# Token order for the row buffers of a gated memory-transformer and FFN kernel: one 128-partition transfer per group in place of two with an outer dimension of 4

## The chip, the core and the metric

The kernel runs on one core of one Trainium2 chip. The metric is device time in microseconds (us) of one execution; several executions are run and their median is taken. All times below are us unless marked otherwise.

The core has a matrix engine (PE, whose weight loads the profile lists as PEld), three engines for elementwise work (DVE, ACT, POOL) and a synchronization engine (SP). DMA transfers are issued here from SP's queue (q1 in the profile) and from ACT's queue (q10); 16 DMA engines carry them out.

## What is computed

Sizes: 2048 tokens of width 640, in 64 segments of 32; 8 memory rows; 32 heads of 192; FFN width 1536. Activations and weights are bf16. Cut to what matters:

```python
g = sigmoid((x * gate_w).sum(-1, keepdims=True))
mem, outs = mem0, []
for s in range(64):
    h = concat([mem, x[32 * s:32 * s + 32]])          # 40 rows
    q, k, v = h @ Wq, h @ Wk, h @ Wv                  # per head
    p = softmax(where(mask, q @ k.T * scale, -1e9))
    o = (p @ v) @ Wo
    mem = o[:8]                                       # feeds the next segment
    outs.append(o[8:])
a = concat(outs)
b = (gelu(x @ w_gate) * (x @ w_up)) @ w_down
out = g * a + (1 - g) * b
```

The memory makes the 64 segments a chain: no segment can start its queries before the last one has its output.

## The kernel before

Everything is written out in program order by a small scheduler (`_Sched`, L50): `add` puts an operation on one engine's list, works out from byte regions what it must wait for, and `emit_stream` (L197) writes each list. An engine's list runs in order, so an operation that waits holds everything behind it on that engine; a DMA's issue belongs to the list of the engine that issues it.

**Stages.** First the FFN for all tokens (L775 to L787), its result stored to a scratch tensor in HBM in plain rows of 128 tokens by one transfer each (L771). Then the queries and keys of the last 8 tokens of every segment, the "left" tokens, which do not depend on the memory, for all segments at once (L796 to L823). Then the 64 segments (`segment`, L1025), each following the list `PROG` (L464): four "octets" of heads, with Q and K projections (`cmode`, L867, matmul L871), evacuation by ACT (L877), transposes (L883), scores and softmax (`scores`, L922: matmul L937, maximum L952, subtraction L954 on DVE, exponential L956 on ACT), V projection (`v_oct`, L898, matmul L905), P transposes, PV and the output projection (`wo_part`, L1011, matmul L1020). A segment ends with the evacuation of the new memory (L1070).

**Weights.** They do not all fit in SBUF. A planner at build time (L501 to L510) keeps 60 of the 84 pieces resident and streams 24 pieces per segment through a ring of five slots, issued in order from SP (`issue_ring`, L544; `piece`, L556) as soon as a slot's last reader is done. Resident pieces whose place is in use early are loaded later: one class after the FFN (L789), another during segment 0 (`load_late`, L573).

**Rows.** Segments come in groups of four (128 tokens; g is the group, q = s % 4 the place in it). One buffer `rowb`, 128 partitions of one token row each (1280 bytes), serves in turn

- the x rows of the next group, loaded in the segment with q = 1 after its second K projection (L1041), transposed in the one with q = 3 (`x_group_transposes`, L658) into `Hx` and used for the gate (`gate_group`, L667) and, segment by segment, by POOL's copies into the segment's input `Hb` (`x_copy`, L699: L701 and L702);
- the FFN rows of this group, loaded in the segment with q = 3 after its third K projection (L1050);
- the output of this group, mixed by DVE in the next group's first segment (`out_group`, L843: L845, L848, L850) and stored from there (`out_store`, L854). The last group's store ends the kernel.

The rows stand in a permuted order: partitions 0 to 95 hold the first 24 tokens of each of the four segments, partitions 96 to 127 the left 8 of each. So `perm_dma` (L638) moves a group by two transfers on ACT's queue, issued at L640, whose HBM side has the outer dimension 4 (segments), then 24 or 8 tokens, then the row. `Hx` and `aT4` (the transposed attention output, filled at L1072 and L1074) have the same order in their columns, and the left tokens of a group are the 32 adjacent columns `Hx[:, k, 96:128]`, which the V projection uses directly (L914).

POOL's list interleaves the copies of the left queries and keys into each octet's Q and K (`left_fill`, L834: L835 and L839) with the x copies.

Of the kernel before, what the change touches and what calls it, by code (L numbers as in the profile page):

```python
# [221 lines left out]
def _build(nc, A_x, A_mem0, A_Wq, A_Wk, A_Wv, A_Wo, seg_len, w_gate, w_up, w_down,  # L222
           gate_w, out, opts=None):
    opts = dict(opts or {})
    Bsz, S, Dm = A_x.shape
    M = A_mem0.shape[1]
    H, Dh = A_Wq.shape[1], A_Wq.shape[2]
    Df = w_gate.shape[1]
    L = int(seg_len)
    assert Bsz == 1 and M == 8 and L == 32 and Dh == 192  # L230
    assert Dm % 128 == 0 and H % 4 == 0 and S % 128 == 0 and Df % 128 == 0
    KT = Dm // 128
# [7 lines left out]
    R = L + M  # L240
    XA = L - M
# [15 lines left out]
    S_ = _Sched(nc)  # L257
    Rg = S_.region
    AUXQ = opts.get("auxq", "act")

    x2 = A_x[0]
    out2 = out[0]
    b_scr = nc.dram_tensor("ffn_b_scratch", (S, Dm), BF, kind="Internal").ap()
# [5 lines left out]
    def al(n):  # L269
        return (n + 63) // 64 * 64  # L270

    wsA = {}
    wsB = {}
    wsA["H"] = al(2 * KT * R * 2)
    wsA["Hx"] = al(KT * 128 * 2)
    wsA["gcol"] = al(2 * 4 * 4)
    wsA["gwT"] = al(KT * 2)
    wsA["ident"] = al(128 * 2)
# [46 lines left out]
    o = wsA_base - wsB_total  # L325
# [6 lines left out]
    o = wsA_base  # L332
    wsA_off = {}
# [3 lines left out]
    o = ffn_base  # L337
# [4 lines left out]
    def bview(o, nbytes, plo=0, phi=128):  # L342
        return arena[plo:phi, o // 2:(o + nbytes) // 2]

    def fview(o, nbytes, plo=0, phi=128):
        return arena[plo:phi, o // 2:(o + nbytes) // 2].bitcast(F32)

    def sreg(o, nbytes, plo=0, phi=128):
        return Rg("sb", o, o + nbytes, plo, phi)

    o_H = wsA_off["H"]
    Hb = [bview(o_H + b * KT * R * 2, KT * R * 2).rearrange("p (k r) -> p k r", r=R) for b in range(2)]
# [2 lines left out]
    o_Hx = wsA_off["Hx"]  # L355
    Hx = bview(o_Hx, KT * 256).rearrange("p (k t) -> p k t", t=128)
    r_Hx = sreg(o_Hx, KT * 256)
    gcol = fview(wsA_off["gcol"], 32)
    r_gcol = [sreg(wsA_off["gcol"] + 16 * b, 16) for b in range(2)]
    gwT = bview(wsA_off["gwT"], KT * 2)  # L360
# [11 lines left out]
    r_mle = sreg(wsA_off["mle"], 32)  # L372
    rowb = bview(wsA_off["rowb"], Dm * 2)
    r_rowb = sreg(wsA_off["rowb"], Dm * 2)
    r_rowbh = [sreg(wsA_off["rowb"], Dm * 2, 0, 4 * XA), sreg(wsA_off["rowb"], Dm * 2, 4 * XA, 128)]
    Qs = bview(wsB_off["Q"], 12 * R * 2).rearrange("p (s r) -> p s r", r=R)
    r_Qm = sreg(wsB_off["Q"], 8)
    r_Ql = sreg(wsB_off["Q"] + 8, 12 * R * 2 - 8)
# [28 lines left out]
    aT4 = bview(wsB_off["aT4"], KT * 256).rearrange("p (k t) -> p k t", t=128)  # L407
# [32 lines left out]
    r_ps = [Rg("ps", b, b + 1) for b in range(8)]  # L440
# [42 lines left out]
    for item in PROG:  # L483
        kind, i = item[0], item[1]
# [33 lines left out]
    o = ring_bytes  # L518
# [9 lines left out]
    o = ring_bytes  # L528
# [71 lines left out]
    def load_residents(cls):  # L600
        for key in order:
# [7 lines left out]
           reads=[r_ident], writes=[r_ident])  # L609
# [3 lines left out]
           reads=[r_e40], writes=[r_e40])  # L613
# [15 lines left out]
    for b in range(8):  # L629
        S_.add("dve", lambda e, b=b: e.memset(ps[:, b, :], 0.0), writes=[r_ps[b]])  # L630

    PP = (slice(0, 4 * XA), slice(4 * XA, 128))

    def rows(ap, g):
        v = ap[128 * g:128 * g + 128, :].rearrange("(s t) d -> s t d", t=L)
        return v[:, 0:XA, :], v[:, XA:L, :]

    def perm_dma(dst, src, reads, writes, sem, watch=False):  # L638
        for i in range(2):
            S_.add(AUXQ, lambda e, i=i: e.dma_start(dst(i), src(i)), reads=reads, writes=writes[i:i + 1],  # L640
                   dma_sem="%s%d" % (sem, i), watch=watch, name=sem)

    def ffn_x_load(blk):
        s = blk % 2
# [4 lines left out]
    S_.add("sp", lambda e: e.dma_start(mem0r[0:M, :], A_mem0[0]), writes=[r_mem0r], dma_sem="mem0")  # L649
    S_.add("sp", lambda e: e.dma_start(gwr[0:KT, :], gate_w.rearrange("(k p) -> k p", p=128)),  # L650
           writes=[r_gwr], dma_sem="gwr")
    perm_dma(lambda i: rowb[PP[i]], lambda i: rows(x2, 0)[i], [], r_rowbh, "rowb")
    ffn_x_load(0)
    S_.add("sp", lambda e: e.dma_start(wg_sb, w_gate.rearrange("(k p) f -> p k f", p=128)), writes=[r_wg], dma_sem="wg")
    S_.add("sp", lambda e: e.dma_start(wu_sb, w_up.rearrange("(k p) f -> p k f", p=128)), writes=[r_wu], dma_sem="wu")
# [3 lines left out]
    def x_group_transposes(g, bk):  # L659
        pv = psb(bk)  # L660
        S_.add("pe", [lambda e, k=k: e.transpose(pv[:, k * 128:(k + 1) * 128], rowb[:, k * 128:(k + 1) * 128], ident)
                      for k in range(KT)],
               reads=[r_rowb, r_ident], writes=[r_ps[bk]], name="xT g%d" % g)
        S_.add("dve", lambda e: e.tensor_copy(out=Hx, in_=pv[:, 0:KT * 128].rearrange("p (k t) -> p k t", t=128)),
               reads=[r_ps[bk]], writes=[r_Hx], name="xT evac g%d" % g)

    def gate_group(g, bk):  # L667
        b = g % 2
# [29 lines left out]

    def x_copy(s):  # L699
        nb, hx, q = s % 2, Hx, s % 4  # L700
        S_.add("pool", [lambda e: e.tensor_copy(out=Hb[nb][:, :, 0:XA], in_=hx[:, :, q * XA:(q + 1) * XA]),  # L701
                        lambda e: e.tensor_copy(out=Hb[nb][:, :, L:R], in_=hx[:, :, 4 * XA + q * M:4 * XA + (q + 1) * M])],  # L702
               reads=[r_Hx], writes=[r_Hxp[nb]], name="x copy s%d" % s)

    def ffn_transposes(blk):
# [146 lines left out]
               reads=[r_ps[bk], r_rowb, r_gcol[g % 2]], writes=[r_rowb], name="mix2 g%d" % g)  # L852

    def out_store(g):  # L854
        perm_dma(lambda i: rows(out2, g)[i], lambda i: rowb[PP[i]], [r_rowb], [], "outw", True)

    OB = 7
    misc = [0]
# [39 lines left out]
    def v_oct(s, o):  # L898
        hb = s % 2
        bank = misc_bank()  # L900
        left = s % 4 == 0
        bank2 = misc_bank() if left else None

        def mms(bk, lhs, k, g_):
            return [lambda e, j=j: e.matmul(  # L905
                ps[32 * j:32 * j + 32, bk, 0:384], lhs, g_[:, 384 * j:384 * (j + 1)],
                start=(k == 0), stop=(k == KT - 1), tile_position=(0, 32 * j)) for j in range(4)]

        for k in range(KT):
            g_, rg_ = piece(s, (2, o, k))  # L910
            S_.add("pe", mms(bank, Hb[hb][:, k, 0:L], k, g_),
                   reads=[rg_, r_Hm[hb], r_Hxp[hb]], writes=[r_ps[bank]], name="V s%d o%d k%d" % (s, o, k))
            if left:
                S_.add("pe", mms(bank2, Hx[:, k, 4 * XA:128], k, g_),  # L914
                       reads=[rg_, r_Hx], writes=[r_ps[bank2]], name="Vl s%d o%d k%d" % (s, o, k))
        S_.add("act", lambda e: e.activation(out=v_sb[o % NVB], in_=ps[:, bank, 0:384], func=ACTF.Copy),  # L916
               reads=[r_ps[bank]], writes=[r_v[o % NVB]], name="V evac s%d o%d" % (s, o))
        if left:
            S_.add("dve", lambda e: e.tensor_copy(out=vl_sb[o], in_=ps[:, bank2, 0:384]),
                   reads=[r_ps[bank2]], writes=[r_vl[o]], name="Vl evac s%d o%d" % (s, o))  # L920
# [104 lines left out]
    def segment(s):  # L1025
        g, q = s // 4, s % 4
        qkbank = {}
        for item in PROG:
            kind, i = item[0], item[1]
            if kind in ("q", "k"):  # L1030
                qkbank[kind] = misc_bank()
                cmode(s, "qk".index(kind), i, qkbank[kind])
                if kind == "q":
                    rows_evac(qkbank["q"])
                if kind == "k" and i == 0 and q == 0 and g > 0:
                    out_group(g - 1, misc_bank())
                if kind == "k" and i == 1:
                    if q == 0 and g > 0:
                        out_store(g - 1)
                    if q == 1 and g + 1 < NG:  # L1040
                        perm_dma(lambda j: rowb[PP[j]], lambda j: rows(x2, g + 1)[j], [], r_rowbh, "rowb")  # L1041
                    if q == 3 and g + 1 < NG:
                        x_group_transposes(g + 1, misc_bank())
                if kind == "k" and i == 2:
                    if s + 1 < NSEG:
                        x_copy(s + 1)
                    if q == 3:
                        if g + 1 < NG:
                            gate_group(g + 1, misc_bank())
                        perm_dma(lambda j: rowb[PP[j]], lambda j: rows(b_scr, g)[j],  # L1050
                                 [Rg("dr", 128 * g, 128 * g + 128)], r_rowbh, "rowb")
            elif kind == "tq":
                row_transp(s, 0, i)
                rows_evac(qkbank["k"])
            elif kind == "tk":
                row_transp(s, 1, i)
            elif kind == "sc":
                scores(s, i)
            elif kind == "v":
                v_oct(s, i)  # L1060
            elif kind == "pt":
                p_transp(s, i)
            elif kind == "pv":
                pv_oct(s, i)
            else:
                wo_part(s, item)
        O3 = ps[:, OB, 0:KT * R].rearrange("p (n r) -> p n r", r=R)
        if s + 1 < NSEG:
            nb = (s + 1) % 2
            S_.add("act", lambda e: e.activation(out=Hb[nb][:, :, XA:L], in_=O3[:, :, XA:L], func=ACTF.Copy),  # L1070
                   reads=[r_ps[OB]], writes=[r_Hm[nb]], name="mem evac s%d" % s)
        S_.add("dve", lambda e: e.tensor_copy(out=aT4[:, :, q * XA:(q + 1) * XA], in_=O3[:, :, 0:XA]),  # L1072
               reads=[r_ps[OB]], writes=[r_aT4], name="aT evac s%d" % s)
        S_.add("dve", lambda e: e.tensor_copy(out=aT4[:, :, 4 * XA + q * M:4 * XA + (q + 1) * M], in_=O3[:, :, L:R]),  # L1074
               reads=[r_ps[OB]], writes=[r_aT4], name="aT evac2 s%d" % s)

    stg_load(0)
# [84 lines left out]
```

## Time and profile before

| | |
|---|---|
| median of 3 runs | 2227.48 us |
| lowest, highest | 2223.69, 2227.95 us |
| span of the profiled execution, first to last instruction | 2220.5 us |
| median less span | 7.0 us |
| mean granted PE clock in the profile | 0.986 |
| bytes moved by DMA in the profile | 642.75 MB |

The profile records one execution; its own time is known by its span only, and what lies around the span (7.0 us) is taken from the median of the runs. Lines such as L640 are lines of the kernel. In the busy digits the span is cut into equal slices, and each digit is a share in tenths; the DMA row is the mean over the 16 DMA engines. A row of the windows view gives start and end of a stretch, its length, each engine's busy time with its count of instructions, the granted PE clock, the DMA share and GB/s; its last row sums all stretches of the call and then gives the means. A row of the source view gives the shortest, median and longest duration in ns. A row of the timeline gives start, duration, engine (with q where it is the engine's queue that issues), line and operation, and in brackets the idle time before it and what ended it.

### The profile page before, as it was taken

What the parts mean: (1) busy time and instruction counts of PE and PEld (TensorE: products, weight loads), DVE (VectorE), ACT (ScalarE), POOL (GpSimd) and SP (SyncE); (2) the same over time, 40 slices, a digit from 0 to 9 for tenths busy, and PEclk for the clock granted to TensorE, in tenths of its full rate; (3) what the DMA queues carried; (4) which work ended last, traced back from release to release, by engine and by line L of the source; (5) the groups of instructions that cost most, each with busy time, mean ns of one, the idle gap of its engine ahead of it and who ended that gap; (6) DMA issues with size and microseconds to landing.
All of it is one profiled execution on the core that took longest, in us unless ns stands there. A gap on an engine that the chain in (4) does not pass through costs nothing.

```text
span 2220.5 us, 94985 instructions
## 1 busy us (share of the span) xinstructions
PE 1912.3 (86%) x41834; PEld 1231.3 (55%) x41862; DVE 943.6 (42%) x3184; ACT 799.7 (36%) x2248; POOL 273.6 (12%) x1210
## 2 busy tenths in 40 slices
PE   7999958888888888888888888888888888888887
PEld 3544425555555555555565655555555655555655
DVE  2222223444444444444444444444444544444444
ACT  2222223334333333343333333333333334333333
POOL 0000001111111111111111111111111111111111
PEclk9999989999999999999999999999999999999999
DMA  9203579999999999999999999999999999999998
GB/s 370 88 13 112 150 236 331 322 303 316 301 318 307 324 303 311 305 316 312 319 320 311 316 300 320 306 313 310 320 302 321 309 322 311 315 315 316 310 309 278
DMA packets 363257, 642.75 MB, mean 289 GB/s; under 512 B 60498, under 2 KB 231770, under 8 KB 362842
## 3 DMA queue, kind: packets, MB, share of 16 engines
q1 hardware_dynamic: 311770, 601.01, 80.2%
q10 hardware_dynamic: 51072, 35.66, 5.4%
q8 instruction: 327, 5.36, 0.9%
q14 instruction: 88, 0.72, 0.1%
HBM read 618.74 MB, written 17.83 MB: 287 GB/s over the span
## 4 chain that ended last, share of the span: by engine, by line
PE 46%; DMA 32%; DVE 14%; ACT 3%; issue 3%; ACTq 2%; SPq 0%; DVEq 0%
PE ps L871 12%; DMA arena<-in_A_Wv_dram 10%; DMA arena<-in_A_Wo_dram 9%; PE ps L1020 9%; DMA arena<-in_A_Wk_dram 8%; PE ps L905 7%; DMA arena<-in_A_Wq_dram 4%; DVE arena L974 4%; PE ps L804 3%; PE ps L883 2%; PE ps L742 2%; PE ps L739 2%; ACTq L819 2%; PE ps L757 2%; DVE ps L954 2%
## 5 line engine op out<-in xcount | busy, mean ns | idle before, releaser
L871 PE MATMUL ps<-arena 128*32 128x384 bf16 x10240 | 488.1, 330 | 69.6 <-DMA arena<-in_A_Wk_dram 23.6
L1020 PE MATMUL ps<-arena 128*128 128x40 bf16 x15360 | 457.9, 180 | 64.8 <-DVE arena L1007 38.1
L1020 PEld LDWEIGHTS ps<-arena 128*128 128x128 bf16 x15360 | 428.9, 96 | 88.8 <-DVE arena L1007 49.5
L871 PEld LDWEIGHTS ps<-arena 128*32 128x32 bf16 x10240 | 247.1, 97 | 254.6 <-DMA arena<-in_A_Wk_dram 63.2
L905 PE MATMUL ps<-arena 128*32 128x384 bf16 x6400 | 324.4, 331 | 53.3 <-DMA arena<-in_A_Wv_dram 30.2
L877 ACT ACTIVATE arena<-ps 128x384 bf16<-128x384 f32 x512 | 249.8, 488 | 181.0 <-PE ps L871 105.1
L974 DVE TENSOR_TENSOR arena<-ps,arena 128x320 bf16<-128x320 bf16 x256 | 125.8, 491 | 387.0 <-PE ps L972 387.0
L835 POOL COPY arena<-arena 128x96 bf16<-128x96 bf16 x256 | 67.4, 263 | 1665.0 <-PE ps L937 1138.3
L956 ACT ACTIVATE ps<-ps 104x160 f32<-104x160 f32 x256 | 71.9, 281 | 494.5 <-DVE ps L954 494.5
L905 PEld LDWEIGHTS ps<-arena 128*32 128x32 bf16 x6400 | 144.6, 96 | 175.5 <-DMA arena<-in_A_Wv_dram 59.2
L883 PE MATMUL ps<-arena 128*128 128x128 bf16 x1536 | 175.9, 223 | 32.0 <-ACT arena L877 31.9
L1001 ACT ACTIVATE arena<-ps 128x320 bf16<-128x320 f32 x256 | 112.3, 439 | 215.4 <-PE ps L993 213.8
L991 PE MATMUL ps<-arena 128*128 128x160 bf16 (+1 forms) x768 | 130.5, 260 | 57.1 <-DVE arena L977 39.6
L916 ACT ACTIVATE arena<-ps 128x384 bf16<-128x384 f32 x256 | 125.6, 491 | 139.0 <-PE ps L905 138.7
L839 POOL COPY arena<-arena 64x32 bf16<-64x32 bf16 (+1 forms) x768 | 165.4, 215 | 47.3
L883 PEld LDWEIGHTS ps<-arena 128*128 128x128 bf16 x1536 | 88.1, 98 | 135.7 <-ACT arena L877 91.1
L952 DVE TENSOR_REDUCE arena<-ps 104x4 f32<-104x160 f32 x256 | 80.9, 316 | 149.3 <-PE ps L937 149.3
L894 ACT ACTIVATE arena<-ps 64x128 bf16<-64x128 bf16 x512 | 136.8, 267 | 6.3
L887 DVE COPY arena<-ps 128x384 bf16<-128x384 bf16 x256 | 89.4, 349 | 102.0 <-PE ps L883 102.0
L993 PE MATMUL ps<-arena 128*128 128x64 bf16 (+1 forms) x768 | 124.5, 202 | 4.0 <-ACT arena L877 4.0
L958 DVE TENSOR_REDUCE arena<-ps 104x4 f32<-104x160 f32 x256 | 83.1, 325 | 99.8 <-ACT ps L956 99.8
L991 PEld LDWEIGHTS ps<-arena 128*128 128x128 bf16 x768 | 72.3, 97 | 91.2 <-DVE arena L977 90.7
(81 smaller groups left out, 1886.3 us busy)
## 6 DMA issues: line engine op xcount, KB each, us to landing
arena<-in_A_Wo_dram SPq DMA_DIRECT2D x591, 320.0 KB, 4.7
arena<-in_A_Wv_dram SPq DMA_DIRECT2D x398, 384.0 KB, 5.2
arena<-in_A_Wk_dram SPq DMA_DIRECT2D x340, 384.0 KB, 5.3
arena<-in_A_Wq_dram SPq DMA_DIRECT2D x276, 384.0 KB, 5.0
left_qk_scratch<-arena ACTq DMA_DIRECT2D x16, 768.0 KB, 8.7
arena<-left_qk_scratch ACTq DMA_DIRECT2D x64, 192.0 KB, 4.6
arena<-in_A_x_dram SPq DMA_DIRECT2D x4, 640.0 KB, 15.0
ffn_b_scratch<-arena ACTq DMA_DIRECT2D x16, 160.0 KB, 1.8
```

Of the source, the lines that this page charges most:

```text
L839: S_.add("pool", lambda e, a=a, b=b, lo=lo, hi=hi, sa=sa: e.tensor_copy(out=Ks[lo:hi, a:b, L:R], in_=stg[lo:hi, o, 1, sa:sa + b - a]), rea ...
L871: S_.add("pe", [lambda e, j=j, k=k, g_=g_: e.matmul(ps[32 * j:32 * j + 32, bank, 0:384], Hb[hb][:, k, 0:L], g_[:, 384 * j:384 * (j + 1)], ...
L877: S_.add("act", lambda e: e.activation(out=rows_sb, in_=ps[:, bank, 0:384], func=ACTF.Copy), reads=[r_ps[bank]], writes=[r_rows], name="ro ...
L883: S_.add("pe", [lambda e, c=c: e.transpose(pv[:, c * 128:(c + 1) * 128], rows_sb[:, c * 128:(c + 1) * 128], ident) for c in range(3)], rea ...
L894: S_.add("act", lambda e, a=a, lo=lo: e.activation(out=Ks[lo:lo + 64, a:a + 4, 0:L], in_=src[lo:lo + 64, 1], func=ACTF.Copy), reads=[r_ps[ ...
L905: return [lambda e, j=j: e.matmul(ps[32 * j:32 * j + 32, bk, 0:384], lhs, g_[:, 384 * j:384 * (j + 1)], start=(k == 0), stop=(k == KT - 1) ...
L916: S_.add("act", lambda e: e.activation(out=v_sb[o % NVB], in_=ps[:, bank, 0:384], func=ACTF.Copy), reads=[r_ps[bank]], writes=[r_v[o % NVB ...
L974: S_.add("dve", lambda e: e.tensor_tensor(out=PTm, in0=apx(pv[:, 512:616], [[64, 2], [0, 4], [1, R]]), in1=apx(mbd, [[0, 2], [1, 4], [0, R]]),
L991: return [lambda e: e.matmul(full, v[:, e0:e0 + 128], PTm[:, ia:ib], start=True, stop=False, skip_group_check=True), lambda e: e.matmul(pa ...
L993: lambda e: e.matmul(part, vl[:, e0:e0 + 128], PTl[:, ia:ib], start=False, stop=True, skip_group_check=True)]
L1001: S_.add("act", lambda e: e.activation(out=apx(u[:, 0, 0, :], [[2 * R, 2], [3 * R, 4], [1, R]]), in_=ps[:, A, 0:2 * W].rearrange("p (c t r ...
L1020: fns.append(lambda e, g_=g_, i=i, c=c, n=n, tl=tl, cc=cc, u=u: e.matmul(ps[:, OB, n * R:(n + 1) * R], g_[:, i, n * 128:(n + 1) * 128], u[ ...
```

## The change

The row buffer, `Hx` and `aT4` now keep token order. A group moves by one transfer over 128 partitions (`row_dma`), with one semaphore in place of two. The left tokens are then no longer adjacent in `Hx`, so a new POOL copy per group collects them in a small buffer `HL` (320 bytes per partition), which the V projection of the left tokens reads. The buffer is taken from the space that the weight planner shares out. Offsets in the x copies and in the evacuations into `aT4` follow.

```diff
+    wsA["HL"] = al(KT * 4 * M * 2)
...
-    r_rowbh = [sreg(wsA_off["rowb"], Dm * 2, 0, 4 * XA), sreg(wsA_off["rowb"], Dm * 2, 4 * XA, 128)]
...
-    PP = (slice(0, 4 * XA), slice(4 * XA, 128))
+    def row_dma(dst, src, reads, writes, sem, watch=False):
+        S_.add(AUXQ, lambda e: e.dma_start(dst, src), reads=reads, writes=writes, dma_sem=sem, watch=watch, name=sem)
     def rows(ap, g):
-        v = ap[128 * g:128 * g + 128, :].rearrange("(s t) d -> s t d", t=L)
-        return v[:, 0:XA, :], v[:, XA:L, :]
-    def perm_dma(dst, src, reads, writes, sem, watch=False):
-        for i in range(2):
-            S_.add(AUXQ, lambda e, i=i: e.dma_start(dst(i), src(i)), reads=reads, writes=writes[i:i + 1],
-                   dma_sem="%s%d" % (sem, i), watch=watch, name=sem)
+        return ap[128 * g:128 * g + 128, :]
...
+        S_.add("pool", lambda e: e.tensor_copy(out=HL.rearrange("p k (s i) -> p k s i", i=M),
+                                               in_=Hx.rearrange("p k (s t) -> p k s t", t=L)[:, :, :, XA:L]),
+               reads=[r_Hx], writes=[r_HL], name="HL g%d" % g)
...
-        S_.add("pool", [lambda e: e.tensor_copy(out=Hb[nb][:, :, 0:XA], in_=hx[:, :, q * XA:(q + 1) * XA]),
-                        lambda e: e.tensor_copy(out=Hb[nb][:, :, L:R], in_=hx[:, :, 4 * XA + q * M:4 * XA + (q + 1) * M])],
+        S_.add("pool", [lambda e: e.tensor_copy(out=Hb[nb][:, :, 0:XA], in_=hx[:, :, q * L:q * L + XA]),
+                        lambda e: e.tensor_copy(out=Hb[nb][:, :, L:R], in_=hx[:, :, q * L + XA:(q + 1) * L])],
...
     def out_store(g):
-        perm_dma(lambda i: rows(out2, g)[i], lambda i: rowb[PP[i]], [r_rowb], [], "outw", True)
+        row_dma(rows(out2, g), rowb, [r_rowb], [], "outw", True)
...
-                S_.add("pe", mms(bank2, Hx[:, k, 4 * XA:128], k, g_),
-                       reads=[rg_, r_Hx], writes=[r_ps[bank2]], name="Vl s%d o%d k%d" % (s, o, k))
+                S_.add("pe", mms(bank2, HL[:, k, :], k, g_),
+                       reads=[rg_, r_HL], writes=[r_ps[bank2]], name="Vl s%d o%d k%d" % (s, o, k))
...
-        S_.add("dve", lambda e: e.tensor_copy(out=aT4[:, :, q * XA:(q + 1) * XA], in_=O3[:, :, 0:XA]),
+        S_.add("dve", lambda e: e.tensor_copy(out=aT4[:, :, q * L:q * L + XA], in_=O3[:, :, 0:XA]),
-        S_.add("dve", lambda e: e.tensor_copy(out=aT4[:, :, 4 * XA + q * M:4 * XA + (q + 1) * M], in_=O3[:, :, L:R]),
+        S_.add("dve", lambda e: e.tensor_copy(out=aT4[:, :, q * L + XA:(q + 1) * L], in_=O3[:, :, L:R]),
```

The calls at the start (x rows of group 0), in the segments with q = 1 and q = 3 and in `out_store` change from `perm_dma` to `row_dma` at the same places.

More of the change, by code (lines that the diff above doesn't have):

```diff
@@ L357, in _build @@
     r_Hx = sreg(o_Hx, KT * 256)
+    HL = bview(wsA_off["HL"], KT * 4 * M * 2).rearrange("p (k t) -> p k t", t=4 * M)
+    r_HL = sreg(wsA_off["HL"], KT * 4 * M * 2)
     gcol = fview(wsA_off["gcol"], 32)
@@ L651, in _build @@
            writes=[r_gwr], dma_sem="gwr")
-    perm_dma(lambda i: rowb[PP[i]], lambda i: rows(x2, 0)[i], [], r_rowbh, "rowb")
+    row_dma(rowb, rows(x2, 0), [], [r_rowb], "rowb")
     ffn_x_load(0)
@@ L1040, in segment @@
                     if q == 1 and g + 1 < NG:
-                        perm_dma(lambda j: rowb[PP[j]], lambda j: rows(x2, g + 1)[j], [], r_rowbh, "rowb")
+                        row_dma(rowb, rows(x2, g + 1), [], [r_rowb], "rowb")
                     if q == 3 and g + 1 < NG:
@@ L1049, in segment @@
                             gate_group(g + 1, misc_bank())
-                        perm_dma(lambda j: rowb[PP[j]], lambda j: rows(b_scr, g)[j],
-                                 [Rg("dr", 128 * g, 128 * g + 128)], r_rowbh, "rowb")
+                        row_dma(rowb, rows(b_scr, g), [Rg("dr", 128 * g, 128 * g + 128)], [r_rowb], "rowb")
             elif kind == "tq":
```

## The prediction

> **What bounds the kernel now.** I read the page first: the busy shares, the DMA digits, the queues and the chain that ended last.
>
> ```profile
> span 2220.5 us, 94985 instructions
> PE 1912.3 (86%) x41834; PEld 1231.3 (55%) x41862; DVE 943.6 (42%) x3184; ACT 799.7 (36%) x2248; POOL 273.6 (12%) x1210
> DMA  9203579999999999999999999999999999999998
> GB/s 370 88 13 112 150 236 331 322 303 316 301 318 307 324 303 311 305 316 312 319 320 311 316 300 320 306 313 310 320 302 321 309 322 311 315 315 316 310 309 278
> q1 hardware_dynamic: 311770, 601.01, 80.2%
> q10 hardware_dynamic: 51072, 35.66, 5.4%
> PE 46%; DMA 32%; DVE 14%; ACT 3%; issue 3%; ACTq 2%; SPq 0%; DVEq 0%
> ...
> 353.00:2186.00 1833.00, 1585.51 (x39141) 1065.56 (x39137) 835.57 (x2957) 702.05 (x2062) 258.51 (x1146) 0.99 0.93 313
> ```
>
> PE is busiest, but a busy PE row includes pipelined and modelled time. From slice 7 on, the transfers are at 9 tenths. The last row, of the windows view, covers segments 1 to 62: PE 1585.5 of 1833 us, DMA share 0.93, 313 GB/s. The chain splits 46% PE, 32% DMA. So the recurrence is bound by both in turns: weights stream through SP's queue (q1) into five ring slots, and whichever of PE and the ring is late ends the wait. ACT (36%) and POOL (12%) have room. What the change touches is small: the row transfers on ACT's queue (q10).
>
> **How the row transfers run today.** The source view of L640, that of L771 (a store of 128 whole rows, the form that the change goes to), and two DMA views: 2217 to 2220.5, which holds the packets of both halves of the final output, and 178.5 to 181, which holds one L771 store alone.
>
> ```profile
> L640 ACTq DMA_DIRECT2D arena<-in_A_x_dram x32: 647/678/1305, 0.8 to 2017.1; - x32
> L640 ACTq DMA_DIRECT2D arena<-ffn_b_scratch x32: 626/643/677, 419.9 to 2196.0; - x32
> L640 ACTq DMA_DIRECT2D out_dram<-arena x32: 650/657/673, 444.7 to 2217.0; - x32
> ...
> L771 ACTq DMA_DIRECT2D ffn_b_scratch<-arena x16: 326/326/399, 51.9 to 181.8; - x16
> ...
> DMA  0000000222312231312222231222110000000000
> q10 hardware_dynamic: 136, 0.16, 14.4%
> ...
> DMA  0000000000003799999630000000000000000000
> q10 hardware_dynamic: 144, 0.16, 18.1%
> ```
>
> Both views move 0.16 MB, 128 rows of 1280 B. The L771 store has 144 packets: 128 rows and 16 short ones, one per DMA engine that reports its end. The split output has 136: 128 rows and 8, so 4 per transfer. The digits say the same: about 0.2 of 16 engines against 0.9. So each half, with its outer dimension of 4, runs on four engines. In time: 14.4% of 16 engines over 3.5 us, divided by 4, is 2.0 us on each of four; 18.1% over 2.5 us is 0.45 us on each of 16. That both halves use the same four follows from this: eight engines would give digits near 5 and end in half the time.
>
> The Trainium skill (DMA: Bandwidth & Descriptors, Why a DMA increments its semaphore by 16 and not by 1) states that a transfer from ACT or SP uses the largest number of engines up to 16 that divides the slowest dimension of both sides, the lowest-numbered ones; the packet counts above agree on 4 and 16, and cannot show the numbers of the engines.
>
> **What a set costs today.** There are 48 sets (two halves each): 16 loads of x (the first at the start, then 15 in segments with s%4=1), 16 loads of FFN rows (s%4=3), 16 stores (15 in s%4=0, one at the end). Segments with s%4=2 have none. I took windows from one memory evacuation (L1070) to the next, and inside them from one softmax exponential (L956) to the next. In order: whole segments s%4=1 (16) and s%4=2 (16); second to third exponential in s%4=1 (16), s%4=2 (16) and s%4=0 (15); third to fourth in s%4=3 (15) and s%4=2 (16).
>
> ```profile
> sum 470.61, PE 400.04 PEld 264.39 DVE 201.55 ACT 179.65 POOL 65.25; mean PE 25.00 PEld 16.52 DVE 12.60 ACT 11.23 POOL 4.08
> sum 453.86, PE 391.00 PEld 263.30 DVE 201.57 ACT 179.03 POOL 65.25; mean PE 24.44 PEld 16.46 DVE 12.60 ACT 11.19 POOL 4.08
> ...
> sum 94.83, PE 79.20 PEld 42.76 DVE 47.34 ACT 42.96 POOL 14.59; mean PE 4.95 PEld 2.67 DVE 2.96 ACT 2.68 POOL 0.91
> sum 81.69, PE 71.64 PEld 40.23 DVE 47.35 ACT 42.44 POOL 14.46; mean PE 4.48 PEld 2.51 DVE 2.96 ACT 2.65 POOL 0.90
> sum 89.81, PE 80.57 PEld 46.02 DVE 52.76 ACT 40.99 POOL 13.86; mean PE 5.37 PEld 3.07 DVE 3.52 ACT 2.73 POOL 0.92
> ...
> sum 75.58, PE 59.65 PEld 45.11 DVE 44.38 ACT 32.84 POOL 2.97; mean PE 3.98 PEld 3.01 DVE 2.96 ACT 2.19 POOL 0.20
> sum 69.41, PE 60.52 PEld 48.62 DVE 47.35 ACT 34.47 POOL 3.10; mean PE 3.78 PEld 3.04 DVE 2.96 ACT 2.15 POOL 0.19
> ```
>
> - s%4=1 does the same arithmetic as s%4=2 and takes 29.41 against 28.37 us: 1.05 more. 0.82 of it (5.93 against 5.11) falls between the second and third exponential, where the weight pieces that travelled beside the x rows are used.
> - s%4=3 issues its load later, and its loss shows one stretch later: 5.04 against 4.34, 0.70 us. (Its other extras, transposes and gate, lie before.)
> - s%4=0: 5.99 against 5.11, but its PE row is longer by 0.89, the extra left-token V matmuls; PE hides the store. I count 0.
>
> Lost to row sets today: 16 x 1.05 + 16 x 0.70 = 28.0 us (the 16 segments with s%4=1 have 15 loads, so the mean already carries that).
>
> **The change part by part.**
>
> *Transfers spread over 16 engines.* A set then adds 0.45 us to every engine instead of 2.0 to four. A ring piece ends when its last engine ends, so the cost goes from "2.0 less what the four were ahead" to at most 0.45. Bounds of what remains: 0, if the ring hides it, and 0.45, if every engine is saturated; the DMA share 0.93 is nearest to the second, so I take 0.45 x 31 sets = 14.0. Gain 28.0 - 14.0 = 14.0 us; with the other end 28.0.
>
> *48 issues fewer.* ACT's queue is held 2 x 0.65 us per set, then 0.33: 1.0 us less. What waits behind it:
>
> ```profile
> 2079.13 1.33 ACTq L640 DMA_DIRECT2D arena<-ffn_b_scratch  x2
> 2080.55 0.28 ACT L956 ACTIVATE ps<-ps 104x160 f32<-104x160 f32 x1 [1.26 <-DVE ps L954]
> ...
> 2080.19 0.33 DVE L954 TENSOR_TENSOR ps<-ps,arena 104x160 f32<-104x160 f32 x1
> ```
>
> The issues end at 2080.46, and the exponential waits for DVE until 2080.52. The cover is only 0.06 us here, but DVE is the later one already, so fewer issues gain nothing: 0. Were the issues longer by more than that, they would show. The consumers wait for one semaphore in place of two, for the same data: 0.
>
> *The HL copy.* One more POOL copy per group, 128x160, behind the evacuation of x^T and ahead of the left fills (L835, L839) and x copies (L701, L702).
>
> ```profile
> L702 POOL COPY arena<-arena 128x40 bf16<-128x40 bf16 x64 | 13.5, 210 | 0.0
> L731 POOL COPY arena<-arena 128x640 bf16<-128x640 bf16 x4 | 2.9, 720 | 88.8 <-DVE arena L723 88.8
> 2076.45 0.21 POOL L702 COPY arena<-arena 128x40 bf16<-128x40 bf16 x1
> ...
> 2079.15 0.32 PEld L937 LDWEIGHTS ps<-arena 128*40 128x40 bf16 x16
> ```
>
> Its price lies between 0.21 and 0.72; by elements about 0.33. The fills behind it are done before the x copies, which end at 2076.66, and PE uses the fills at 2079.15: 2.5 us of cover, so 0. Without that cover it would cost 15 x 0.33 = 5 us, at most 15 x 0.72 = 11. V's left matmuls (L914) read HL a segment after it was written, 32 columns as before, and the next write of Hx waits for HL only a group later. Evacuations into aT4 and x copies keep their shapes; only offsets move: 0.
>
> *320 bytes per partition.* The planner's arithmetic leaves 2,688 bytes to spare before and 2,368 after: 24 streamed pieces a segment in both, the same ones. One Wv piece moves from the loads inside segment 0 to those right after the FFN. At 313 GB/s, 384 KB are 1.25 us; the segment-0 side waits for transfers, the other does less so: between 0 and 1.25 of gain, I take 0.5.
>
> *The end.* The last store is on the path.
>
> ```profile
> 2216.32 1.35 ACTq L640 DMA_DIRECT2D out_dram<-arena  x2
> 178.44 0.33 ACTq L771 DMA_DIRECT2D ffn_b_scratch<-arena  x1
> ```
>
> Its packets end with the 30th slice of the 2217 view, at 2219.6. The lone L771 store, issued at 178.44, ends its packets with the 21st slice of its view, at 179.81, 1.37 us after the issue. Issued at 2216.32, that form ends at 2217.7: gain 1.9 us, and little can hide or add to it, since nothing else runs.
>
> **Sum**: 14.0 + 0.5 + 1.9 = 16.4 us of the profiled execution's 2220.5. The runs' median, 2227.48, is 7.0 above the span; that part I leave unchanged. 2227.5 - 16.4 = 2211.1.
>
> **Rivals.**
>
> *Only the end moves.* If the transfers share a limit other than their engines, or the 1.05 and 0.70 have another cause, spreading buys nothing in the recurrence. Against: slice 1 of the page moves 370 GB/s where the recurrence has 313, so a shared limit isn't reached, and two separate stretches lose where their rows travel. For: the two stretches are differences of means that hold other waits too. Time: 2227.5 - 1.9 = 2225.6. The Trainium skill speaks for this one (DMA: Bandwidth & Descriptors, Rules for kernel authors): two transfers to disjoint halves of the partitions serialize on the same 16 engines, so joining them saves little more than the issue; the digits of the last store, 2 where one store shows 9, disagree for this form.
>
> *The four engines set the pace throughout.* If the ring ran against them in every segment, each set would give back 2.0 - 0.45 = 1.55 us: 47 x 1.55 + 2.4 = 75 us, 2152. For: a group of four segments takes 1833 / 62 x 4 = 118 us and has three sets, so a mean DMA share of 0.93 puts those four at 0.93 + 3 x 1.55 / 118 = 0.97. Against: s%4=2, without a set, is only 1.05 shorter, and s%4=0 loses nothing.
>
> *An engine that the rows don't use today is the slowest.* Then its load grows by 0.45 us per set in the 31 sets that meet a bound ring, 14.0, and nothing comes back from the four: 2227.5 + 14.0 - 1.9 = 2239.6, slower. It decides when the slowest of the other twelve is more than 2.0 us behind the four at a set. Against: then the sets would cost nothing today, and the same stretches say 0.70 to 1.05.
>
> **How the numbers follow.** A measurement can tell about 0.2% (4.5 us) from no change. Forecast (gain 5 to 31 us, centre 16): 0.62. Only the end: 0.19. Four engines throughout: 0.09. Slower: 0.10. The range runs from the forecast's best, 28.0 + 1.25 + 1.9 = 31 us or 2196, to no change, 2228, and leaves out the last two, 0.19. Faster: 0.62 + 0.09 + 0.01 of "only the end"; same 0.18; slower 0.10.
>
> **What would show it.** Right: 144 packets per row set and digits near 9 in the last store; L1070 to L1070 in s%4=1 within 0.5 us of s%4=2, most of it back between the second and third exponential; s%4=3 shorter by 0.2 to 0.7 in its later stretch; s%4=0 unchanged; the tail shorter by 1.9. Wrong: the 1.05 still there with one transfer per set (another cause), a longer s%4=2 (the slow-engine rival), a shorter s%4=2 and s%4=0 (four engines throughout), or POOL's fills later than PE.

## The result, and the profile after

| | before | changed |
|---|---|---|
| median of 5 runs | 2223.8 us | 2209.5 us |
| lowest, highest | 2221.49, 2227.95 | 2205.03, 2216.85 |
| span of the profiled execution | 2220.5 | 2215.1 |

The ratio of changed to before is 0.9943, 95% interval [0.9921, 0.9966]. Later batches of the changed kernel gave 0.9910 [0.9888, 0.9932] and 0.9920 [0.9892, 0.9948], and 0.9897 [0.9872, 0.9922] in e2 below, which turned out to be the same kernel. So it is faster by 13 to 23 us; 16.4 was forecast. The profiled execution of the changed kernel took 2216.85, the slowest of its five runs, so its whole stages are read with care here, and a second profile of it is put beside it below.

The page after:

```profile
span 2215.1 us, 94949 instructions
PE 1915.8 (86%) x41862; PEld 1234.7 (56%) x41862; DVE 943.5 (43%) x3184; ACT 799.0 (36%) x2248; POOL 278.7 (13%) x1226
DMA  9204589999999999999999999999999999999998
...
q1 hardware_dynamic: 311770, 601.01, 80.8%
q10 hardware_dynamic: 51456, 35.66, 5.3%
```

The same bytes move on q10, with 384 more packets: 48 sets now have 16 short packets each in place of 8. PE and the weight stream on q1 stay the two bounds.

The source view of the row transfers, and the DMA view from 2212.5 to 2216, which holds the last store:

```profile
L635 ACTq DMA_DIRECT2D arena<-in_A_x_dram x16: 339/340/388, 0.8 to 2011.4; - x16
L635 ACTq DMA_DIRECT2D arena<-ffn_b_scratch x16: 326/326/327, 419.3 to 2192.4; - x16
L635 ACTq DMA_DIRECT2D out_dram<-arena x16: 344/344/345, 442.8 to 2212.8; - x16
...
DMA  0000000000000288999200000000000000000000
q10 hardware_dynamic: 144, 0.16, 13.2%
```

One issue of 0.34 us in place of two of 0.65; 144 packets, 128 rows and 16 ends; 8 to 9 tenths of the engines busy for half a microsecond where 2 tenths were busy for two.

The same windows as in the prediction, in the same order, but without the whole segments: second to third exponential in s%4=1, 2 and 0, then third to fourth in s%4=3 and 2.

```profile
sum 80.71, PE 71.27 PEld 40.30 DVE 47.35 ACT 42.41 POOL 14.37; mean PE 4.45 PEld 2.52 DVE 2.96 ACT 2.65 POOL 0.90
sum 80.96, PE 72.09 PEld 40.38 DVE 47.35 ACT 42.52 POOL 14.54; mean PE 4.51 PEld 2.52 DVE 2.96 ACT 2.66 POOL 0.91
sum 89.27, PE 80.16 PEld 45.80 DVE 52.76 ACT 40.98 POOL 13.70; mean PE 5.34 PEld 3.05 DVE 3.52 ACT 2.73 POOL 0.91
...
sum 66.43, PE 58.17 PEld 45.22 DVE 44.38 ACT 32.65 POOL 3.14; mean PE 3.88 PEld 3.01 DVE 2.96 ACT 2.18 POOL 0.21
sum 70.01, PE 61.09 PEld 48.56 DVE 47.34 ACT 34.57 POOL 3.10; mean PE 3.82 PEld 3.04 DVE 2.96 ACT 2.16 POOL 0.19
```

The two local losses are gone. s%4=1 takes 80.71 / 16 = 5.04 us where it took 5.93, as much as s%4=2 (5.06). s%4=3 takes 66.43 / 15 = 4.43 where it took 5.04, against 4.38 in s%4=2. s%4=0, 5.95 after 5.99, has hardly moved.

Yet the recurrence of this one execution is no shorter. The windows from the first to the last memory evacuation, in the profile before, this one, and a second profile of the changed kernel (from the last batch below):

```profile
353.48:2185.74 1832.26, 1585.06 (x39121) 1065.21 (x39121) 835.57 (x2957) 701.85 (x2062) 258.51 (x1146) 0.99 0.93 313
```

```profile
347.76:2183.11 1835.35, 1587.91 (x39121) 1068.98 (x39121) 835.50 (x2957) 701.24 (x2062) 263.30 (x1161) 0.99 0.94 313
```

```profile
348.66:2163.81 1815.15, 1582.77 (x39121) 1065.60 (x39121) 835.65 (x2957) 701.55 (x2062) 263.27 (x1161) 0.99 0.94 316
```

1832.3, 1835.4 and 1815.2: two profiled executions of the changed kernel differ by 20 us here. The stretch where a row set travels nearly repeats (5.04 and 5.13 in s%4=1); the sum of all ring waits does not. So the sum is taken from medians of runs in the experiments, and the place from the stretches.

What the three rows do show alike is when the recurrence begins: 5.7 and 4.8 us earlier than before. The FFN's start is 1.5 us of it. First matmul of the FFN, and the landing of the first weights, before and after:

```profile
13.89 1.44 PE L739 MATMUL ps<-arena 128*128 128x512 bf16 x3 [1.21 <-DVE arena L723]
arena<-in_B_w_gate_dram SPq DMA_DIRECT2D x1, 1920.0 KB, 10.3
```

```profile
12.39 2.29 PE L739 MATMUL ps<-arena 128*128 128x512 bf16 x5 [1.21 <-DVE arena L723]
arena<-in_B_w_gate_dram SPq DMA_DIRECT2D x1, 1920.0 KB, 8.8
```

The first row set travels beside these weights; with it on four engines w_gate lands 1.5 us later.

The last left store is issued earlier and is shorter too. Timelines of both, ACT's and SP's queues:

```profile
292.54 2.25 SPq L597 DMA_DIRECT2D arena<-in_A_Wv_dram  x4
292.80 17.15 ACTq L819 DMA_DIRECT2D left_qk_scratch<-arena  x4
```

```profile
289.36 1.80 SPq L599 DMA_DIRECT2D arena<-in_A_Wv_dram  x3
289.67 15.79 ACTq L819 DMA_DIRECT2D left_qk_scratch<-arena  x4
```

Three Wv pieces, not four, are loaded beside the store whose data segment 0 reads back: its four issues hold ACT's queue 1.4 us less. That is the piece that the 320 bytes moved out of segment 0. So of the 5.7 us by which the recurrence begins earlier here, 3.1 lie before this store (1.5 of them at the FFN's start), 1.4 in it and 1.2 behind it.

And the end:

```profile
2212.84 0.34 ACTq L635 DMA_DIRECT2D out_dram<-arena  x1
```

From the last issue to the end of the span it is 2215.1 - 2212.8 = 2.3 us; before, from 2216.32 to 2220.5, it was 4.2.

### The profile page after: what moved, and what is told of

It reads as the page before. It is cut to its first block, busy times and chain, and to the rows that moved or that the text cites. A ratio compares the mean times of both kernels' runs of the same rounds, so it can differ in the third digit from the quotient of the medians.

```text
span 2215.1 us, 94949 instructions
## 1 busy us (share of the span) xinstructions
PE 1915.8 (86%) x41862; PEld 1234.7 (56%) x41862; DVE 943.5 (43%) x3184; ACT 799.0 (36%) x2248; POOL 278.7 (13%) x1226
## 3 DMA queue, kind: packets, MB, share of 16 engines
q10 hardware_dynamic: 51456, 35.66, 5.3%
## 4 chain that ended last, share of the span: by engine, by line
PE 34%; DMA 32%; DVE 13%; issue 2%; ACT 2%; SPq 0%; DVEq 0%
PE ps L871 12%; DMA arena<-in_A_Wo_dram 12%; DMA arena<-in_A_Wk_dram 10%; PE ps L1020 8%; PE ps L905 7%; DMA arena<-in_A_Wv_dram 6%; DMA arena<-in_A_Wq_dram 5%; DVE arena L974 4%; PE ps L883 2%; PE ps L991 2%; DVE ps L954 2%; DVE arena L977 2%; ACT arena L877 1%; DVE arena L952 1%; DVE arena L1007 1%
```

## The experiments

Two theories went in. **Spread**: four engines carry a set for 2.0 us each, the ring piece beside it ends late, and that is the gain in the recurrence. **Issue or layout**: one issue and one semaphore in place of two, or the moved piece, is the gain; or all of it lies at start and end. Kernels of one batch ran on the same chip, each with the kernel before beside it (medians 2221.8, 2221.1 and 2223.8 in the three batches).

### Batch 1

`e1_after_again`, the changed kernel unchanged.

> The changed kernel once more, unchanged, because the profiled execution of it was the slowest of its five (span 2215.1 us) and its segments from the first to the last memory evacuation took 1835.4 us, 3.1 more than before, while the medians differ by 14.3 us. Theory A (four engines cost time throughout the recurrence): in a profile nearer to the median the stretch between the first and the last memory evacuation is 8 us or more shorter than the 1832.3 of before. Theory B (only the start and the end gain, the gain within the recurrence is given back at later ring waits): that stretch stays within 4 us of 1832.3, and start and end together are 8 us shorter. Time by both: 2205 to 2217.

Measured: 2201.45, ratio 0.9910 [0.9888, 0.9932]. Its profiled recurrence took 1817.0 us against 1832.3 before: theory A's figure, 15 less. But theory B's other figure is nearly met as well: the recurrence begins 4.7 us earlier than before, and what follows its last memory evacuation is 2.3 us shorter (32.5 against 34.7), 7 us together. So the gain lies in both. And one profile decides little: e2's, of the same kernel, has 1825.7.

`e2_token_order_four_engines`:

```diff
-        return ap[128 * g:128 * g + 128, :]
+        return ap[128 * g:128 * g + 128, :].rearrange("(s t) d -> s t d", t=L)
```

> The changed kernel, with token order, one transfer per group, the HL copy and the shifted SBUF layout, but the HBM side of every row transfer written with an outer dimension of 4, so that it runs on four engines as before. Theory A (the spread is what gains): as slow as before, 2219 to 2228, 132 packets per set. Rival (one issue and one semaphore in place of two, or the layout, is what gains): as fast as the changed kernel, 2205 to 2214.

Measured: 2201.37, ratio 0.9897 [0.9872, 0.9922]. It seemed to kill the spread theory. It did not, because the edit made no difference. ACT's queue of this run:

```profile
q10 hardware_dynamic: 51456, 35.66, 5.4%
```

51456 packets is the count of the changed kernel, 144 a set, so the transfers use 16 engines. The rows are adjacent, and 4 x 32 of them can be written as one dimension of 128; that this merging took place is the likely reason, not one that the trace shows. So this is a second run of the changed kernel. Its median agrees within 0.1 us, which is luck: the ratios differ by 0.0013, 3 us, and each is known to about 5 us.

`e3_two_more_loads_16` and `e4_two_more_loads_4`, an added row load after the first and third K projection of every segment (the main lines of e3's edit; e4 has e2's order in it):

```diff
+    wsA["dum"] = al(Dm * 2)
...
+                if kind == "k" and i in (0, 2):
+                    row_dma(dum, rows(x2, g), [], [r_dum], "dum")
```

> The changed kernel with two more row loads in every segment (128 in all) into a buffer that nobody reads, 128 partitions over 16 engines. It measures the remaining price of a spread set. Saturated engines: 128 x 0.45 = 58 us more than the changed kernel, 2268. Half hidden: 2238. Hidden wholly by the ring: within 8 us of 2210.

> The same two more row loads per segment, with an outer dimension of 4, on four engines. It measures the price of a set in the old form. By the stretches of before, 0.70 to 1.05 us per set that meets a bound ring (three of four segments): 96 x 0.70 to 96 x 1.05 = 67 to 101 us over the changed kernel, 2277 to 2311; if the four engines set the pace throughout, 128 x 2.0 = 256 us, 2466; if four engines are as good as 16, the time of the 16-engine form within 5 us.

Measured: 2235.29, ratio 1.0067 [1.0039, 1.0095], and 2234.78, ratio 1.0048 [1.0018, 1.0078]. e4 has e3's packets, so both are the 16-engine form. 33.8 us over e1 for 128 sets is 0.26 us a set: nearest to "half hidden".

### Batch 2

Here the order of the rows cannot be merged: the outer dimension has step 1 row, the inner 4 rows.

`e5_four_engines`:

```diff
-        return ap[128 * g:128 * g + 128, :]
+        return ap[128 * g:128 * g + 128, :].rearrange("(t s) d -> s t d", s=4)
```

> The changed kernel, one transfer per set, but the HBM side visits the 128 rows of a group in an order with an outer dimension of 4 that cannot be merged (step 1 row outside, 4 rows inside), for x loads, FFN-row loads and stores alike. The tokens of a group are therefore permuted (the output's values are not the reference's); the work is the same. 132 packets per set show four engines (the earlier attempt kept rows adjacent, was merged, and ran on 16: it was the changed kernel again). Spread theory: most of the gain is gone, 2214 to 2224, and the second to third exponential in s%4=1 is back near 5.9 us. Issue or layout theory: 2199 to 2206, like the changed kernel.

Measured: 2220.53, ratio 0.9998 [0.9974, 1.0022]: no gain over before is left, with token order, HL, the layout and one issue per set all kept. Its queue, its stretches (second to third exponential in s%4=1, third to fourth in s%4=3), and the landing of w_gate:

```profile
q10 hardware_dynamic: 50880, 35.66, 5.5%
...
sum 95.01, PE 77.88 PEld 42.36 DVE 47.33 ACT 43.05 POOL 14.51; mean PE 4.87 PEld 2.65 DVE 2.96 ACT 2.69 POOL 0.91
sum 75.24, PE 59.18 PEld 44.55 DVE 44.37 ACT 33.06 POOL 3.02; mean PE 3.95 PEld 2.97 DVE 2.96 ACT 2.20 POOL 0.20
...
arena<-in_B_w_gate_dram SPq DMA_DIRECT2D x1, 1920.0 KB, 10.3
```

576 packets fewer than the changed kernel: 48 sets with 4 ends in place of 16. 95.01 / 16 = 5.94 and 75.24 / 15 = 5.02 are the numbers of before (5.93, 5.04), and w_gate lands at 10.3 again. Three places, one cause. The edit also visits rows in steps of 4 in place of adjacent ones; the kernel before visits adjacent rows on four engines and has the same stretches, so the step is not what costs.

`e6_two_more_loads_true_4`, e3 with that order for the added loads (the end of the kernel also waits for them).

> The changed kernel with two more row loads in every segment into a buffer that nobody reads, in the order with an outer dimension of 4 that cannot be merged: four engines. The 16-engine form of the same loads took 2235, 34 us over the changed kernel, 0.26 us a set. Spread theory: 0.70 to 1.05 us for each set that meets a bound ring, 96 of 128: 2268 to 2302. Four engines setting the pace throughout: over 2400. If the spread is worth nothing: 2235 again, within 6.

Measured: 2316.92, ratio 1.0413 [1.0383, 1.0442]. Queue of e3, then of e6:

```profile
q10 hardware_dynamic: 69888, 56.64, 8.3%
```

```profile
q10 hardware_dynamic: 68352, 56.63, 8.2%
```

128 sets with 12 ends fewer each is the difference of 1536. By the ratios, (1.0413 - 1.0067) x 2222 = 77 us for 128 sets: 0.60 us a set more on four engines than on 16. With e3's 0.26 a four-engine set costs 0.86. It is far from the 2.0 a set that "the four engines set the pace throughout" asks for.

`e7_before_with_320_bytes_less`:

```diff
     wsA["Hx"] = al(KT * 128 * 2)
+    wsA["HL"] = al(KT * 4 * M * 2)
```

> The kernel before with the 320 bytes per partition of HL reserved and not used, nothing else: one Wv piece moves from the loads inside segment 0 to those after the FFN. Layout theory: it gains the part of the start that lies after the left projections, about 1.2 us (one piece of 384 KB), the recurrence as before: 2218 to 2223 beside 2221.8. If the layout is behind the gain in the recurrence too: 2202 to 2212.

Measured: 2216.10, ratio 0.9975 [0.9950, 1.0000]. It lies below the range given for the piece alone, 0 to 11 us under the kernel before. Its timeline has three Wv pieces ahead of the last left store, as in the changed kernel, and the source view of its memory evacuation gives the first and the last:

```profile
289.18 1.80 SPq L598 DMA_DIRECT2D arena<-in_A_Wv_dram  x3
L1071 ACT ACTIVATE arena<-ps x63: 204/204/205, 347.8 to 2171.6; 128x40 bf16<-128x40 f32 x63
```

The recurrence begins at 347.8, 5.7 us earlier than before, though the row sets still use four engines and w_gate lands at 10.3. Its last left store is issued at 289.49 and holds the queue 15.90 us, so 3.3 of the 5.7 lie before the store and 1.25 in it. All profiles with the piece moved begin the recurrence between 347.6 and 349.9. The kernel before has one profile only, so how much of the 5 us is the piece, and how much that one execution, stays open. The recurrence itself took 1823.8 us here, 8 less than before, which is within what two profiles of one kernel differ by; e5, which has the layout too, took 1837.7, so a gain by the layout there isn't seen. The second to third exponential in s%4=1 took 5.62 and the third to fourth in s%4=3 4.70, so the loss is still there, but smaller than in the other two profiles on four engines.

`e8_two_halves_of_64_rows`:

```diff
+    r_rowbh = [sreg(wsA_off["rowb"], Dm * 2, 64 * i, 64 * i + 64) for i in range(2)]
...
-        S_.add(AUXQ, lambda e: e.dma_start(dst, src), reads=reads, writes=writes, dma_sem=sem, watch=watch, name=sem)
+        for i in range(2):
+            S_.add(AUXQ, lambda e, i=i: e.dma_start(dst[64 * i:64 * i + 64], src[64 * i:64 * i + 64]), reads=reads,
+                   writes=[r_rowbh[i]] if writes else [], dma_sem="%s%d" % (sem, i), watch=watch, name=sem)
```

> The changed kernel with each row set moved by two transfers of 64 adjacent rows, each on 16 engines, with two issues and two semaphores as before. Spread theory: as fast as the changed kernel but for the second issue at the very end, 2200 to 2206. Issue theory (ACT's queue held longer is what cost): most of the gain is gone, 2214 to 2222.

Measured: 2213.62, ratio 0.9961 [0.9937, 0.9985]: between the two expectations, and this chip had not run the changed kernel. On what the second issue costs it is inconclusive, so it was repeated beside the changed kernel. On the engines it says more: beside e5 on the same chip, with the same token order, HL and layout and one issue more per set, it is 6.9 us faster, and the intervals of their ratios overlap by 0.0011 only.

### Batch 3

`f1_after_same_chip`, the changed kernel; `f2_two_halves_again`, e8 again.

> The changed kernel again, so that the three beside it have it on the same chip. So far 2209.5 in one batch and 2201.4 in another, with 2223.8 and 2221.8 for the kernel before. If a batch moves the two forms differently by up to 8 us, this one lies between 2199 and 2212, and then the 2213.6 of the two halves of 64 rows must be read against this number and not against 2201.4.

> Two transfers of 64 rows per set, on 16 engines each. Spread theory (spreading is the whole gain): within 4 us of the changed kernel beside it, of which 1 to 2 us are the second issue at the end. Rival (the second issue and semaphore cost time in the recurrence too, some 0.2 us a set): 8 to 14 us above it.

Measured: 2204.95, ratio 0.9920 [0.9892, 0.9948], and 2206.60, ratio 0.9937 [0.9909, 0.9964]. 1.7 us apart, as spread alone says, but each is known to about 6 us. The issues of f2, from its source view:

```profile
L637 ACTq DMA_DIRECT2D arena<-in_A_x_dram x32: 493/589/891, 0.8 to 2000.8; - x32
L637 ACTq DMA_DIRECT2D arena<-ffn_b_scratch x32: 458/552/1057, 417.5 to 2180.0; - x32
L637 ACTq DMA_DIRECT2D out_dram<-arena x32: 497/562/1291, 441.7 to 2202.2; - x32
```

ACT's queue is held 1.1 us per set, nearly the 1.3 of before, and no cost beyond the noise is seen in this pair. Why e8 read 2213.6 on another chip stays open; against the changed kernel's ratios, 0.9897 to 0.9943, its 0.9961 is 4 to 14 us more, so a small cost of the second issue isn't excluded.

`f3_stores_on_four`, the order of e5 for the 15 stores inside the recurrence only:

```diff
+        dst = rows(out2, g)
+        if g < NG - 1:
+            dst = dst.rearrange("(t s) d -> s t d", s=4)
```

> The changed kernel with the 15 output stores inside the recurrence (not the last one) in the order with an outer dimension of 4 that cannot be merged, on four engines; the output rows of 15 groups are permuted. The prediction counts nothing for the stores, because PE bounds the segments with s%4=0: within 3 us of the changed kernel. If every set counts alike: 15 of 46 sets, 4 to 7 us above it.

Measured: 2200.00, ratio 0.9908 [0.9880, 0.9937], 5 us under the changed kernel beside it and inside its interval. Its queue:

```profile
q10 hardware_dynamic: 51276, 35.66, 5.5%
```

180 packets fewer than the changed kernel, 15 stores with 12 ends fewer each: they did run on four engines. No loss from the stores is seen.

`f4_no_row_transfers`:

```diff
-                    if q == 0 and g > 0:
-                        out_store(g - 1)
-                    if q == 1 and g + 1 < NG:
-                        row_dma(rowb, rows(x2, g + 1), [], [r_rowb], "rowb")
...
-                        row_dma(rowb, rows(b_scr, g), [Rg("dr", 128 * g, 128 * g + 128)], [r_rowb], "rowb")
+                        if g + 1 == NG:
+                            row_dma(rowb, rows(b_scr, g), [Rg("dr", 128 * g, 128 * g + 128)], [r_rowb], "rowb")
```

> The changed kernel without the 45 row transfers inside the recurrence: no x loads after the first group, no FFN-row loads and no stores before the last group; the gate, mixing and copies run on stale rows. It shows what the spread sets still cost. At 0.26 us a set, as the added loads cost: 12 us under the changed kernel. At 0.45 a set in 30 loads: 14. If the ring hides spread sets: within 4 us.

Measured: 2198.14, ratio 0.9890 [0.9860, 0.9919]: 6.8 us under the changed kernel, 0.15 us a set, with intervals that overlap. What is left to gain from the row transfers is about that. No version tried that does the whole work is faster than the changed kernel beyond the noise.

## Why the prediction was right, step by step

**Spread over 16 engines, 14.0 us.** Right in kind. With everything else of the change kept, four engines give the time of before (e5), 6.9 us above the spread form on the same chip (e8), and the two local losses return. e6 against e3 shows the same far outside the noise: 0.0346 apart in the ratio, each known to 0.003.

Its size is known only roughly. e5's ratio less those of the changed kernel in the other batches, 0.9897 to 0.9943, times 2222, is 12 to 22 us; less 1.5 at the start and 1.9 at the end, 9 to 19 remain for the recurrence. By e5 less e8, 6.9 us, less 1.9 at e8's own start and end, it is 5. From the other side, the whole gain of 13 to 23 less about 7 at start and end is 6 to 16. 14.0 is inside most of these.

Part of that is luck, since its two halves were both too large. The loss of today was put at 28.0 us. Against f4, which has no row transfers in the recurrence, it is (0.9998 - 0.9890) x 2222 = 24 from e5, less 3.4 about 21, and (1 - 0.9890) x 2222 = 24 from before, less 8.6 at f4's earlier start and shorter end about 16. What remains after the change was put at 0.45 a set, 14.0 in all; f4 says 0.15 a set, 6.8 in all, e3 0.26 a set. A DMA share of 0.93 was read as saturated, and the ring still hides half or more.

One step that made the loss too large is the whole-segment difference of s%4=1 and s%4=2, 1.05. It is no measure of a set. Whole segments s%4=1 and 2 in the changed kernel's first profile, then in f1's, then f1's second to third exponential in both:

```profile
sum 467.28, PE 395.71 PEld 265.15 DVE 201.58 ACT 179.08 POOL 65.27; mean PE 24.73 PEld 16.57 DVE 12.60 ACT 11.19 POOL 4.08
sum 459.71, PE 395.41 PEld 265.87 DVE 201.54 ACT 179.24 POOL 65.28; mean PE 24.71 PEld 16.62 DVE 12.60 ACT 11.20 POOL 4.08
...
sum 464.10, PE 395.76 PEld 264.12 DVE 201.63 ACT 179.25 POOL 65.26; mean PE 24.73 PEld 16.51 DVE 12.60 ACT 11.20 POOL 4.08
sum 446.76, PE 392.44 PEld 263.64 DVE 201.65 ACT 179.18 POOL 65.26; mean PE 24.53 PEld 16.48 DVE 12.60 ACT 11.20 POOL 4.08
...
sum 82.07, PE 73.11 PEld 40.92 DVE 47.37 ACT 42.67 POOL 14.37; mean PE 4.57 PEld 2.56 DVE 2.96 ACT 2.67 POOL 0.90
sum 80.80, PE 72.21 PEld 40.37 DVE 47.36 ACT 42.53 POOL 14.56; mean PE 4.51 PEld 2.52 DVE 2.96 ACT 2.66 POOL 0.91
```

Divided by 16, the segments differ by 0.47 in one profile of the changed kernel and by 1.08 in the other, and by 0.58 in e5's, on four engines. So the sign "within 0.5 us" held in one profile and failed in another, and means little. The stretch, 5.13 against 5.05, shows the loss gone in both profiles: 0.82 and 0.70 were the better measure, though e7's 5.62 says that they vary too. And even the stretches give 0.89 and 0.61 back, 16 x 0.89 + 15 x 0.61 = 23 us, more than any figure for the recurrence above: it seems that later ring waits take a part of it again, which no run shows directly.

**48 issues fewer, 0.** Not contradicted: f2 holds ACT's queue almost as long as before and stands within 1.7 us of the changed kernel, which is what its second issue and transfer can cost at the very end. With e8's reading open, it is shown only to a few us.

**HL copy, 0.** Right, at its size too: about 0.33 was read from its neighbours.

```profile
L663 POOL COPY arena<-arena 128x160 bf16<-128x160 bf16 x16 | 5.1, 316 | 205.4 <-DVE arena L661 205.4
```

That it costs nothing is read from the changed kernel's timeline, the copy, the last fill behind it and PE's next use of the fills:

```profile
2070.93 0.32 POOL L663 COPY arena<-arena 128x160 bf16<-128x160 bf16 x1 [11.61 <-DVE arena L661]
2071.70 0.77 POOL L839 COPY arena<-arena 128x64 bf16<-128x64 bf16 x3
2074.52 0.32 PEld L937 LDWEIGHTS ps<-arena 128*40 128x40 bf16 x16
```

The fills end at 2072.47, 2.0 us before PE needs them.

**320 bytes, 0.5.** The right piece, but too small. The last left store alone is shorter by 17.15 - 15.79 = 1.4 us, above the upper bound of 1.25. With nothing else changed (e7), the recurrence began 5.7 us earlier in the profile and the median was 5.0 us lower, with 0 to 11 by the interval. How much of that is the piece stays open.

**The first set, not priced.** This step was wrong: the load of x "at the start" was counted among the sets and then left out of the sum. It costs 1.5 us: w_gate lands that much later beside it on four engines, and the first FFN matmul starts that much later. With the piece, the start gave 4.7 to 5.7 us where 0.5 was in the sum. A start that was priced too low and a recurrence that was probably priced too high then make a sum near the middle of the measured 13 to 23, which is luck in part.

**The end, 1.9.** Measured 4.2 - 2.3 = 1.9.

**The rivals.** "Only the end moves" falls with e5 and e6, though start and end together are worth 7 us, about a third to a half of the gain. The Trainium skill's rule beside it, on two transfers to disjoint halves of the partitions (DMA: Bandwidth & Descriptors, Rules for kernel authors), agrees with f2 within the noise, 1.7 us for halves of 64 rows, and not with the halves of before, because those did not use all engines. "Four engines throughout" falls with e6: 0.86 us a set, not 2.0. "A slow engine among the other twelve" asked for a time above that of before; nothing of it is seen.

## What to carry to other kernels

Count the packets of a small transfer alone in a window: rows plus one short packet per engine used shows how many of the 16 engines it has, and a transfer on four can hold up a large one that it meets, where the end of that one is waited for: here the loads of x and of FFN rows did, and the stores beside a longer PE stretch did not (f3). Price such a meeting in the stretch where the large transfer's data is used, against the same stretch without it, and take sums over a ring-bound stage from medians of many runs on one chip, not from one profile. Sets at the start and at the end, where nothing else covers them, are worth a sum of their own.

## What the runs showed of the hardware beyond that

An outer dimension of 4 is not by itself a transfer on four engines: where the rows are adjacent (e2) the packets are those of 16 engines, 144 a set. The Trainium skill (DMA: Bandwidth & Descriptors, Why a DMA increments its semaphore by 16 and not by 1) goes by the slowest dimension as the instruction carries it; that agrees, if the adjacent rows are merged before. And the issue on ACT's queue has a price by form: 0.34 us for one transfer of 128 partitions (changed kernel), 0.55 to 0.59 for one of 64 (f2), 0.65 for the 96 and 32 with an outer dimension (before), so cutting a set in two more than triples its issue time.
